# One maximum for the second layer's input, a second accumulator for the last block, and row sums for the first weight matrix

## The chip, the core and the metric

The kernel runs on one core of one Trainium2 chip. The metric is the device time of one execution in microseconds (us). A core has five engines that run on their own and meet through semaphores: TensorE (PE, with its weight loads PEld), VectorE (DVE), ScalarE (ACT), GpSimd (POOL) and SyncE (SP, which only issues transfers here).

## The reference

The input x has 2 sequences of 4096 tokens with 192 features. A causal convolution over 7 tokens, whose taps are a softmax over one row of weights per head, is followed by two feed-forward layers of width 2048: the first with a sigmoid-approximated GELU, the second with a rational function P/Q.

```python
w = exp(weight - max(weight)); w = w / (sum(w) + 1e-9)      # 8 heads, 7 taps
x = einsum('hk,bskhg->bshg', w, x_unf)                      # 8192 x 192
h = x @ w_in1;  g = h / (1 + exp(-1.702 * h));  x2 = g @ w_out1
h = x2 @ w_in2
P = a0 + a1*h + a2*h**2 + a3*h**3
Q = 1 + abs(b0)*abs(h) + abs(b1)*h**2
out = (P / (Q + 1e-6)) @ w_out2
```

All weights of the two layers, the taps' softmax and both layers belong to the program. The weight matrices come as 64-bit floats and are turned into 32-bit ones on DVE.

## The kernel before, in words

The 8192 tokens are worked on in 16 blocks of 512. A block's 512 x 192 input is held transposed as one tile of 128 x 768: 512 columns with features 0 to 127 (bank 0 where it is in PSUM, the accumulators) and 256 columns in which features 128 to 191 of the two halves of the block stand above each other (bank 1). Precision comes from splitting: a 32-bit operand is scaled by a power of two and kept as a high and a low 16-bit part, and a product is three 16-bit products (`TERMS`). So before a layer's input can be split, the largest magnitude in it has to be known: DVE makes a maximum per partition, PE spreads it over all partitions with a small matmul (`all_max`, L85), DVE takes the maximum of that (L89) and makes the power of two (`scales`, L78 to L348), ACT writes the high part (`high`, L333), DVE the low part (`low`, L336). For x2, the second layer's input, four more small DVE operations (`x2_scales`, L343) make the factors of the polynomial in between.

The loop is a software pipeline. Phase j (0 to 14) has a front phase and a back phase. In the front phase block j + 1 goes through the first layer's input product (`h_product(0, ...)`: 12 matmuls of `h_main`, L400, and 12 of `h_side`, L413) and its GELU (ACT, L491; POOL and DVE split the result, L501 and L507), while block j goes through the second layer's input product (`h_product(1, ...)`) and the parts of the rational function (`unit`, L544 to L547; `denominator`, L552). In the back phase PE makes block j + 1's first-layer output, x2: all `o1_main` matmuls (L463, into bank 0), then all `o1_side` matmuls (L473, into bank 1 of the same tile). Meanwhile ACT takes logarithms (L558) and then inverses (L562) of block j's denominators, DVE multiplies them in (`quotient`, L566), and POOL makes the convolution of a block further ahead (`x_conv_pool`: per tap a pair of multiplications, L326, and an addition, L330) in phases 0 to 12. The second layer's output, `o2_chunk` (L452), takes one quotient's half at a time; three chunks of a block stand in the back phase, the other 13 are spread over the next front phase (`late_pe`).

The order on each engine is the order in which this code issues the instructions; no scheduler changes it. PSUM has two pools: `ps_h`, three tiles that all input products and small matmuls share in turn, and `ps_o`, one tile. x2 of a block and the output of a block take turns in that one tile: the output may start when x2 has been split, and the next x2 when the output has been copied out by `store`.

In the back phase before (L684 to L721), `x2_red(n1, 0)` takes the maximum of bank 0 after the main matmuls, and `x2_red(n1, 1)` that of bank 1 after the side matmuls; `x2_red_end` (L517) joins them. The tracker of waits goes by tiles. `all_max` stands between the two halves of the next block's `h_main` (L425 to L428). The four first quotients follow the low part.

`last_phase` (L607) works on block 15 alone: `units` makes products and polynomial, with the leftover chunks of block 14 in between, `store(j - 1)` copies block 14's output out, and only then may `own(i)`, block 15's chunks, go into the same `ps_o` tile. Five units come ahead of the first logarithms.

`prologue` (L723) loads and converts the weights. For the first matrix (three pieces) DVE makes `w_max` per piece (L195); for the others ACT makes row sums of magnitudes (`w_sum`, L203), which bound the maximum from above. `softmax_taps` (L111) stands between two steps of the first piece.

## Time and profile before

| what | us |
|---|---|
| median of three runs | 1273.59 |
| the runs | 1272.25, 1273.59, 2085.2 |
| profiled execution | 1266.0 |
| its span, first to last instruction | 1264.0 |
| mean granted TensorE clock in it | 0.993 |

The profile is of one execution. Times in it count from the span's start. A matmul in 32 bits shows as two records and its end is modelled, so starts are the better measure of PE's steps. In brackets behind a row stands how long the engine was idle before it and what ended that.

### The profile page before, as it was taken

How to read it: one execution, taken by the hardware profiler on the slowest of the kernel's cores; microseconds unless marked ns; L12 is line 12 of the kernel's file. 1: busy time of each engine (PE TensorE's matmuls, PEld its weight loads, DVE VectorE, ACT ScalarE, POOL GpSimd, SP SyncE). 2: the span in 40 equal slices, each digit the busy share in tenths (PEclk: the TensorE clock that was granted, in tenths of full speed). 3: DMA queues.
4: the chain of work that ended last, by engine and by line, in shares of the span. 5: the costliest groups of instructions: out<-in, count | busy, mean ns of one | idle time of the engine just before them, and what ended most of it. 6: DMA issues, size and time to landing. Idle time of an engine off the chain costs nothing.

```text
span 1264.0 us, 24525 instructions
## 1 busy us (share of the span) xinstructions
PE 1204.1 (95%) x10762; PEld 959.3 (76%) x10762; DVE 1049.3 (83%) x1095; ACT 828.0 (66%) x825; POOL 495.7 (39%) x400
## 2 busy tenths in 40 slices
PE   5999999999999999999999999999999999999897
PEld 3547686887868688786878868687886868788686
DVE  7888898797979879797987979799797979879485
ACT  3625857668585765858576585867658576775774
POOL 2023725427272454727345272734527263112000
PEclk9999999999999999999999999999999999999898
DMA  8710001000010001000010000100000000000000
GB/s 236 236 25 2 1 1 26 1 27 1 1 27 1 26 1 27 2 1 26 1 26 2 26 1 2 26 1 26 2 19 8 1 14 1 13 1 14 1 14 13
DMA packets 32947, 27.88 MB, mean 22 GB/s; under 512 B 10485, under 2 KB 32073, under 8 KB 32073
## 3 DMA queue, kind: packets, MB, share of 16 engines
q1 hardware_dynamic: 32248, 26.31, 7.3%
q8 instruction: 84, 1.38, 0.5%
q14 instruction: 22, 0.18, 0.0%
q10 hardware_dynamic: 593, 0.01, 0.0%
HBM read 18.97 MB, written 6.29 MB: 20 GB/s over the span
## 4 chain that ended last, share of the span: by engine, by line
PE 84%; DVE 12%; ACT 2%; issue 2%; DMA 1%; ACTq 0%; DVEq 0%
PE po L452 25%; PE ph L400 23%; PE po L463 13%; PE ph L413 12%; PE po L473 7%; DVE pp L566 3%; DVE sc L343 1%; PE pc L316 1%; DVE xs L336 1%; PE pm L85 1%; DVE v L167 1%; DVE red L512 1%; PE pt L270 1%; DVE v L176 1%; DVE top L89 1%
## 5 line engine op out<-in xcount | busy, mean ns | idle before, releaser
L501 POOL TENSOR_SCALAR hl<-g,sc 128x1024 f16<-128x1024 f32 x120 | 210.8, 1756 | 540.1 <-ACT g L491 540.1
L400 PE MATMUL ph<-xs,wm 128*128 128x256 f16 x3072 | 382.2, 274 | 3.5 <-ACT xs L333 2.2
L400 PEld LDWEIGHTS <-wm 128*128 128x128 f16 x3072 | 287.3, 98 | 75.2 <-issue 38.4
L452 PE MATMUL po<-wo,pp 128*128 128x192 f32 x1920 | 331.9, 328 | 9.5 <-DVE pp L566 9.5
L452 PEld LDWEIGHTS po<-wo,pp 128*128 128x128 f32 x1920 | 311.5, 191 | 13.7 <-PE ph L400 8.3
L491 ACT ACTIVATE g<-ph,sc 128x1024 f32<-128x1024 f32 x120 | 133.7, 1114 | 176.3 <-PE ph L413 176.1
L544 ACT ACTIVATE qq<-ph,sc 128x1024 f32<-128x1024 f32 x128 | 142.5, 1113 | 158.2 <-PE ph L400 85.6
L552 DVE SCALAR_TENSOR_TENSOR qq<-qq,ab 128x1024 f32<-128x1024 f32 x128 | 209.5, 1637 | 0.0
L413 PE MATMUL ph<-xs,wr 64*128 64x256 f16 x3072 | 194.6, 271 | 0.8 <-DVE xs L336 0.8
L507 DVE SCALAR_TENSOR_TENSOR hl<-g,sc,hl 128x1024 f16<-128x1024 f32 x120 | 180.4, 1503 | 0.0
L566 DVE SCALAR_TENSOR_TENSOR pp<-pp,ab,qq 128x1024 f32<-128x1024 f32 x120 | 179.5, 1525 | 0.0
L546 DVE TENSOR_TENSOR pp<-pp,ph 128x1024 f32<-128x1024 f32 x120 | 145.5, 1212 | 39.4 <-ACT pp L545 39.4
L413 PEld LDWEIGHTS <-wr 64*128 64x128 f16 x3072 | 138.1, 94 | 47.4 <-issue 33.0
L463 PE MATMUL po<-hl,wo 128*128 128x512 f16 x720 | 157.8, 379 | 0.0
L547 DVE SCALAR_TENSOR_TENSOR pp<-pp,sc,ph 128x1024 f32<-128x1024 f32 x120 | 153.7, 1281 | 4.3
L330 POOL TENSOR_TENSOR xc<-xc,tap 128x768 f32<-128x768 f32 x78 | 152.6, 1956 | 6.5
L558 ACT ACTIVATE qq<-qq,eps,ab 128x1024 f32<-128x1024 f32 x128 | 146.9, 1228 | 3.4 <-DVE qq L552 3.2
L545 ACT ACTIVATE pp<-ph,sc 128x1024 f32<-128x1024 f32 x120 | 143.8, 1198 | 0.2 <-PE po L452 0.2
L463 PEld LDWEIGHTS <-wo 128*128 128x128 f16 x720 | 70.3, 98 | 81.7
L562 ACT ACTIVATE qq<-qq 128x1024 f32<-128x1024 f32 x128 | 124.5, 1046 | 0.2
L326 POOL TENSOR_SCALAR tap<-xt,wt 128x512 f32<-128x512 f32 (+1 forms) x156 | 101.4, 662 | 6.4
L473 PE MATMUL po<-hl,wo 128*64 128x256 f16 x1440 | 81.5, 273 | 21.6 <-DVE red L512 21.6
(96 smaller groups left out, 700.1 us busy)
## 6 DMA issues: line engine op xcount, KB each, us to landing
raw<-in_moe_w_out_dram SPq DMA_DIRECT2D x8, 768.0 KB
out_dram<-on SPq DMA_DIRECT2D x15, 384.0 KB
xn<-in_x_dram SPq DMA_DIRECT2D x16, 256.0 KB
raw<-in_moe_w_in_dram SPq DMA_DIRECT2D x4, 1024.0 KB
xn<-in_x_dram SPq DMA_DIRECT2D x32, 64.0 KB
raw<-in_moe_w_in_dram SPq DMA_DIRECT2D x4, 512.0 KB
wr<-wr SPq DMA_DIRECT2D x8, 128.0 KB
out_dram<-on SPq DMA_DIRECT2D x2, 192.0 KB
```

Source lines behind the costliest of these rows:

```text
L330: nc.gpsimd.tensor_tensor(out=flat_of(c), in0=flat_of(c), in1=flat_of(d), op=ALU.add)
L400: nc.tensor.matmul(out=ph[:, h, k * TH:(k + 1) * TH], lhsT=wm[m][:, a_, f], rhs=xs[:, b_, h * TH:(h + 1) * TH], start=(start and k == 0 an ...
L413: nc.tensor.matmul(out=ph[:, h, k * TH:(k + 1) * TH], lhsT=wr[m][rows, a_, other, f], rhs=xs[rows, b_, T:W], start=(start and other == 0 a ...
L452: nc.tensor.matmul(out=dst, lhsT=tokens(t, k, g // 2)[:, g % 2 * P:(g % 2 + 1) * P], rhs=rhs, start=(done == 0 and g % 2 == 0 and q == 0), ...
L463: nc.tensor.matmul(out=po_t[0, n][:, 0].rearrange("p (h t) -> p h t", h=2), lhsT=w[:, 0:P], rhs=all_tokens(t, k), start=(at == 1 and q == ...
L473: nc.tensor.matmul(out=po_t[0, n][h * D2:(h + 1) * D2, 1, 0:TH], lhsT=w[:, P:D], rhs=tokens(t, k, h), start=(at == 1 and q == 0), stop=(at ...
L501: nc.gpsimd.tensor_scalar(out=hl[:, 0], in0=g, scalar1=sc1_t[n][:, 4:5], scalar2=1.0, op0=ALU.mult, op1=ALU.mult)
L507: nc.vector.scalar_tensor_tensor(out=hl[:, 1], in0=g, scalar=sc1_t[n][:, 4:5], in1=hl[:, 0], op0=ALU.mult, op1=ALU.subtract)
L547: nc.vector.scalar_tensor_tensor(out=pp, in0=pp, scalar=sc[:, 5:6], in1=h, op0=ALU.add, op1=ALU.mult)
L552: nc.vector.scalar_tensor_tensor(out=qq, in0=qq, scalar=ab[:, 14:15], in1=qq, op0=ALU.add, op1=ALU.mult)
L558: nc.scalar.activation(out=qq, in_=qq, func=ACTF.Ln, scale=ab[:, 15:16], bias=eps)
L566: nc.vector.scalar_tensor_tensor(out=pp, in0=pp, scalar=ab[:, 0:1], in1=qq, op0=ALU.add, op1=ALU.mult)
```

## The change

Four things, in the order of the program.

1. Prologue: `softmax_taps` is issued ahead of the first weight piece, and the three maxima of the first matrix (`w_max` on DVE) become row sums (`w_sum` on ACT).
2. Back phase: the two maxima of x2 and the operation that joins them become one maximum over all 768 columns, after the side matmuls. `x_scales` and `x_scale_out` of the next x move ahead of the side matmuls. The first four inverses and the first quotient move ahead of the maximum. `all_max` moves from the middle of `h_main` to its end.
3. In the back phase of block 14 (where there is no next block) ACT copies x2 out of PSUM first; maximum, high and low part read the copy, and the first chunk of block 14's output goes ahead of `all_max`.
4. `last_phase`: block 15's output gets a tile of its own from `ps_h`. Leftover chunks are spread anew, the first logarithms are of four units instead of five, own chunks come ahead of `store(j - 1)`.

```diff
     def h_product(m, n, i, between=None):
...
-            h_main(*at, start=True, chunks=(0,))
+            h_main(*at, start=True)
             if between is not None:
                 between()
-            h_main(*at, chunks=(1,))
             h_side(*at, stop=True)
...
-        if done == 0:
+        if (m, n) not in po_t:
             po_t[m, n] = ps_o.tile([P, 2, 512], F32, tag="o", name="po")
...
+    def x2_red(src):
+        red = tiny.tile([P, 1], F32, tag="red2", name="red2")
+        nc.vector.tensor_reduce(out=red, in_=flat_of(src), axis=AX.X, op=ALU.max, apply_absolute_value=True)
+        return red
...
         def units(i, late=0):
             pp = hl_tile().rearrange("p two t -> p (two t)").bitcast(F32)
             unit(j, h_product(1, j, i), pp)
-            if i < first:
-                late_step(j - 1, i)
+            late_step(j - 1, i)
...
-        first = NS // 2 + 1
-        for i, late in enumerate((0, 0, 2, 5)):
+        first = NS // 2
+        for i, late in enumerate((0, 0, 2, 1, 2, 2)):
             units(i, late)
-        units(first - 1, len(late_pe))
         each(log, j, range(first))
+        units(first + 2, 1)
+        each(inverse, j, range(first))
+        each(quotient, j, range(first - 1))
+        units(first + 3, len(late_pe))
+        quotient(j, first - 1)
+        po_t[1, j] = ps_tile("po")
+        for i in range(first):
+            own(i)
         store(j - 1)
-        for i in range(first):
+        each(log, j, range(first, NS))
+        for i in range(first, NS):
             inverse(j, i)
             quotient(j, i)
-        units(first), units(first + 1)
-        own(0)
-        units(first + 2)
-        for i in range(1, first):
-            own(i)
-        quotients(range(first, NS))
         for i in range(first, NS - 1):
             own(i)
...
     def back_phase(j, n1, n2, conv, splits):
...
-        for i in range(NS):
-            o1_product(o1_main, n1, i, splits[i])
-            log(j, i)
-        if conv is not None:
-            x_max(conv)
-        x2_red(n1, 0, red)
-        for i in range(NS):
-            o1_product(o1_side, n1, i, splits[i])
-        if conv is not None:
-            x_scales(conv)
-            x_scale_out(conv)
-        x2_red(n1, 1, red)
-        x2_red_end(red)
+        for part in (o1_main, o1_side):
+            for i in range(NS):
+                o1_product(part, n1, i, splits[i])
+                if part is o1_main:
+                    log(j, i)
+            if part is o1_main and conv is not None:
+                x_max(conv)
+                x_scales(conv)
+                x_scale_out(conv)
+        chunks = [lambda i=i, k=k: o2_chunk(j, i, k) for i in range(NS) for k in range(2)]
+        each(inverse, j, (0, 1, 2, 3))
+        quotient(j, 0)
+        src = po_t.pop((0, n1))
...
+        if n2 is None:
+            copy = p1.tile([P, 2, T], F32, tag="xc", name="copy")
+            nc.scalar.activation(out=flat_of(copy), in_=flat_of(src), func=ACTF.Copy)
+            src = copy
+        red = x2_red(src)
+        if n2 is None:
+            chunks.pop(0)()
+            all_max(red, pm)
+        else:
+            early[n2, 0] = h_product(0, n2, 0, lambda: all_max(red, pm))
             early[n2, 1] = h_product(0, n2, 1)
...
-        x2_split(n1, sc, sc1_t.pop(n1)[:, 6:7])
-        each(quotient, j, (0, 1, 2, 3))
+        x2_split(n1, src, sc, sc1_t.pop(n1)[:, 6:7])
+        each(quotient, j, (1, 2, 3))
...
+        softmax_taps()
         w_high(("in", 0, 0))
-        softmax_taps()
...
-        w_max(("in", 0, 0), red[:, 0:1])
+        w_sum(("in", 0, 0), red[:, 0:1])
```

On PE, in a steady back phase, after the last main matmul, where `pm` is the tile of the next x's maximum. Before:

```order
L463 MATMUL po<-hl_2092,wo_82 128x512
L85 MATMUL pm<-ident,red 128x128 [waits Activation_49]
L473 LDWEIGHTS wo_82
L473 MATMUL po<-hl_1617,wo_82 64x256 [waits DVE_49]
L473 LDWEIGHTS wo_82
```

Now:

```order
L457 MATMUL po<-hl_2091,wo_82 128x512
L85 MATMUL pm<-ident,red 128x128 [waits Activation_49]
L467 LDWEIGHTS wo_82
L467 MATMUL po<-hl_1616,wo_82 64x256
L467 LDWEIGHTS wo_82
```

The order is the same (L473 is now L467); the first side matmul's wait for DVE is gone.

On DVE, in the same back phase, from the next x's scale (`sc_2201`, then `sc_2199`) to the quotients; `sc_2311` belongs to x2. Before:

```order
L348 TENSOR_SCALAR sc_2201<-sc_2201 128x1 [waits DVE_49]
L512 TENSOR_REDUCE red_2141<-po 128x1
L343 TENSOR_SCALAR sc_2201<-sc_2201,cst 128x1
...
L343 TENSOR_SCALAR sc_2201<-sc_2201,cst 128x1 [waits DVE_49]
L512 TENSOR_REDUCE red_2141<-po 128x1 [waits PE_49]
L517 TENSOR_SCALAR red_2141<-red_2141 128x1 [waits DVE_49]
L89 TENSOR_REDUCE top<-pm_2310 128x1 [waits PE_49]
...
L343 TENSOR_SCALAR sc_2311<-ab,sc_2311 128x3 [waits DVE_49]
...
L336 SCALAR_TENSOR_TENSOR xs_2372<-po,sc_2311,xs_2372 128x768 [waits Activation_49]
L566 SCALAR_TENSOR_TENSOR pp<-pp,ab,qq 128x1024 x4
```

Now:

```order
L338 TENSOR_SCALAR sc_2199<-sc_2199,cst 128x1 [waits DVE_49]
L557 SCALAR_TENSOR_TENSOR pp<-pp,ab,qq 128x1024 [waits Activation_49]
L507 TENSOR_REDUCE red_2312<-po 128x1 [waits PE_49]
L89 TENSOR_REDUCE top<-pm_2310 128x1 [waits PE_49]
...
L338 TENSOR_SCALAR sc_2311<-ab,sc_2311 128x3 [waits DVE_49]
...
L331 SCALAR_TENSOR_TENSOR xs_2370<-po,sc_2311,xs_2370 128x768 [waits Activation_49]
L557 SCALAR_TENSOR_TENSOR pp<-pp,ab,qq 128x1024 x3
```

One quotient (L566, now L557) has moved ahead of the maximum (L512, now L507), which is one row where there were three.

On ACT, at the turn from block 14 to block 15, from the first inverses of block 14 to the first pass over block 15. Before:

```order
L562 ACTIVATE qq<-qq 128x1024 [waits Activation_49] x4
L333 ACTIVATE xs_12806<-po,sc_12795 128x768 [waits DVE_49,PE_49]
L562 ACTIVATE qq<-qq 128x1024 [waits Activation_49] x4
L544 ACTIVATE qq<-ph,sc_12795 128x1024 [waits DVE_49,PE_49,Activation_49]
L545 ACTIVATE hl_12834<-ph,sc_12795 128x1024
```

Now:

```order
L553 ACTIVATE qq<-qq 128x1024 [waits Activation_49] x4
L691 ACTIVATE copy<-po 128x768 [waits PE_49]
L328 ACTIVATE xs_12785<-copy,sc_12769 128x768 [waits DVE_49,Activation_49]
L553 ACTIVATE qq<-qq 128x1024 x4
L535 ACTIVATE qq<-ph,sc_12769 128x1024 [waits DVE_49,PE_49]
```

The copy stands behind the four inverses, and the high part (L333, now L328) reads it.

## Rows read from the trace of the kernel before

**Rows 1.** The page, busy times: share of the span and instructions of each engine.
```profile
PE 1204.1 (95%) x10762; PEld 959.3 (76%) x10762; DVE 1049.3 (83%) x1095; ACT 828.0 (66%) x825; POOL 495.7 (39%) x400
```
**Rows 2.** Waits of PE: who was waited for, us in total, times, longest.
```profile
PE po L473 <- DVE red L512: 21.6, 15, 1.5
```
**Rows 3.** Timeline of PE, one back phase: start, length, line, tile, count, idle before.
```profile
442.11 5.43 PE L473 MATMUL po<-hl,wo 128*64 128x256 f16 x96 [1.55 <-DVE red L512]
447.47 0.83 PE L400 MATMUL ph<-xs,wm 128*128 128x256 f16 x6
448.31 0.49 PE L85 MATMUL pm<-ident,red 128*128 128x128 f32 x2
...
450.14 1.49 PE L400 MATMUL ph<-xs,wm 128*128 128x256 f16 x12
451.56 1.49 PE L413 MATMUL ph<-xs,wr 64*128 64x256 f16 x24
...
454.90 3.33 PE L452 MATMUL po<-wo,pp 128*128 128x192 f32 x19 [0.44 <-DVE pp L566]
```
**Rows 4.** Timeline of PE, the turn to the last block and the end.
```profile
1188.93 6.09 PE L452 MATMUL po<-wo,pp 128*128 128x192 f32 x24 [4.28 <-DVE pp L566]
...
1228.96 2.84 PE L452 MATMUL po<-wo,hl 128*128 128x192 f32 x16 [1.80 <-DVE hl L566]
...
1249.55 10.40 PE L452 MATMUL po<-wo,hl 128*128 128x192 f32 x48 [5.16 <-DVE hl L566]
```
**Rows 5.** Timeline of ACT, inverses in that phase and in phase 14.
```profile
443.74 3.90 ACT L562 ACTIVATE qq<-qq 128x1024 f32<-128x1024 f32 x4
...
1181.83 2.93 ACT L562 ACTIVATE qq<-qq 128x1024 f32<-128x1024 f32 x3
```
**Rows 6.** Timeline of POOL, the phase of rows 3.
```profile
444.35 1.14 POOL L326 TENSOR_SCALAR tap<-xt,wt 128x512 f32<-128x512 f32 x2
445.58 1.82 POOL L330 TENSOR_TENSOR xc<-xc,tap 128x768 f32<-128x768 f32 x1
```
**Rows 7.** Timeline of DVE, the same phase and the x maximum after it.
```profile
447.58 0.42 DVE L512 TENSOR_REDUCE red<-po 128x1 f32<-128x256 f32 x1 [4.91 <-PE po L473]
...
449.84 0.71 DVE L343 TENSOR_SCALAR sc<-ab,sc 128x3 f32<-128x3 f32 x1
...
450.99 1.01 DVE L336 SCALAR_TENSOR_TENSOR xs<-po,sc,xs 128x768 f16<-128x768 f32 x1
451.92 2.84 DVE L566 SCALAR_TENSOR_TENSOR pp<-pp,ab,qq 128x1024 f32<-128x1024 f32 x1
...
479.79 0.94 DVE L358 TENSOR_REDUCE red<-xn 128x1 f32<-128x768 f32 x1
```
**Rows 8.** Timeline of DVE, phase 14, where POOL rests.
```profile
1185.96 0.47 DVE L343 TENSOR_SCALAR sc<-sc 128x2 f32<-128x2 f32 x2
...
1187.50 4.86 DVE L566 SCALAR_TENSOR_TENSOR pp<-pp,ab,qq 128x1024 f32<-128x1024 f32 x4
```
**Rows 9.** Timeline of DVE, first back phase, two operations that met POOL.
```profile
142.26 1.71 DVE L552 SCALAR_TENSOR_TENSOR qq<-qq,ab 128x1024 f32<-128x1024 f32 x1
...
153.79 2.11 DVE L343 TENSOR_SCALAR sc<-sc 128x2 f32<-128x2 f32 x2
```
**Rows 10.** Timeline of POOL, first back phase.
```profile
141.36 2.96 POOL L326 TENSOR_SCALAR tap<-xt,wt 128x512 f32<-128x512 f32 x2
...
153.82 1.81 POOL L330 TENSOR_TENSOR xc<-xc,tap 128x768 f32<-128x768 f32 x1
```
**Rows 11.** One stretch: us, busy PE, PEld, DVE, ACT, POOL, granted clock, DMA, GB/s.
```profile
1189.00:1195.00 6.00, 6.00 (x26) 5.77 (x28) 3.37 (x3) 1.32 (x2) 0.00 (x0) 0.68 0.00 0
```
**Rows 12.** The beginning: the taps' transfer in the chain, and DVE's timeline.
```profile
4.39 5.58 DMA wt<-in_weight_dram
...
9.01 0.69 DVE L164 TENSOR_SCALAR u<-raw 128x1024 uint32<-128x1024 uint32 x1 [0.44 <-DMA raw<-in_moe_w_in_dram]
...
13.48 1.22 DVE L195 TENSOR_REDUCE wred<-v 128x1 f32<-128x1024 f32 x1
```

More of the change, by code (lines that the diff above doesn't have):

```diff
@@ L616, in units, with own @@
             denominator(j, i)
-        def quotients(steps):
-            each(log, j, steps)
-            for i in steps:
-                inverse(j, i)
-                quotient(j, i)
-        def own(i):
+        def own(i, groups=range(NG)):
             for k in range(2):
-                o2_chunk(j, i, k)
-        first = NS // 2 + 1
-        for i, late in enumerate((0, 0, 2, 5)):
+                o2_chunk(j, i, k, groups)
+        first = NS // 2
+        for i, late in enumerate((0, 0, 2, 1, 2, 2)):
             units(i, late)
-        units(first - 1, len(late_pe))
         each(log, j, range(first))
+        units(first + 2, 1)
[6 more added lines that the diff above has]
+            own(i)
         store(j - 1)
-        for i in range(first):
+        each(log, j, range(first, NS))
+        for i in range(first, NS):
             inverse(j, i)
             quotient(j, i)
-        units(first), units(first + 1)
-        own(0)
-        units(first + 2)
-        for i in range(1, first):
-            own(i)
-        quotients(range(first, NS))
         for i in range(first, NS - 1):
@@ L645, in last_phase @@
         for groups in (range(0, 2), range(2, 4)):
-            for k in range(2):
-                o2_chunk(j, NS - 1, k, groups)
+            own(NS - 1, groups)
         store_half(j, 0)
@@ L675, in front_phase, with x2_split @@
         return splits
-    def x2_split(n, sc, unit):
+    def x2_split(n, src, sc, unit):
         xs = xs_t[1, n] = p2.tile([P, 2, W], F16, tag="xs2", name="xs2")
-        po = po_t.pop((0, n))
-        high(po, sc[:, 1:2], xs)
+        high(src, sc[:, 1:2], xs)
         x2_scales(sc, unit)
-        low(po, sc[:, 1:2], xs)
+        low(src, sc[:, 1:2], xs)
     def back_phase(j, n1, n2, conv, splits):
@@ L689, in back_phase @@
                 x_conv_pool(conv, k)
-        red = tiny.tile([P, 3], F32, tag="red2", name="red2")
-        for i in range(NS):
-            o1_product(o1_main, n1, i, splits[i])
-            log(j, i)
-        if conv is not None:
-            x_max(conv)
-        x2_red(n1, 0, red)
-        for i in range(NS):
-            o1_product(o1_side, n1, i, splits[i])
-        if conv is not None:
-            x_scales(conv)
-            x_scale_out(conv)
-        x2_red(n1, 1, red)
-        x2_red_end(red)
+        for part in (o1_main, o1_side):
[11 more added lines that the diff above has]
+        src = po_t.pop((0, n1))
         pm = ps_tile("pm2")
         sc = sc2_t[n1] = tiny.tile([P, 24], F32, tag="sc2", name="sc2")
-        if n2 is not None:
-            early[n2, 0] = h_product(0, n2, 0, lambda: all_max(red[:, 2:3], pm))
+        if n2 is None:
[8 more added lines that the diff above has]
+            early[n2, 0] = h_product(0, n2, 0, lambda: all_max(red, pm))
             early[n2, 1] = h_product(0, n2, 1)
-        else:
-            all_max(red[:, 2:3], pm)
-        each(inverse, j, (0, 1, 2, 3))
         scales(pm, sc)
-        x2_split(n1, sc, sc1_t.pop(n1)[:, 6:7])
-        each(quotient, j, (0, 1, 2, 3))
+        x2_split(n1, src, sc, sc1_t.pop(n1)[:, 6:7])
+        each(quotient, j, (1, 2, 3))
         each(inverse, j, (4, 5, 6, 7))
-        chunks = [lambda i=i, k=k: o2_chunk(j, i, k) for i in range(NS) for k in range(2)]
         if n2 is not None:
@@ L756, in prologue @@
             more()
-            w_max(("in", 0, c), red[:, c:c + 1])
+            w_sum(("in", 0, c), red[:, c:c + 1])
         w_scale(red, 3, 0)
@@ L838, in prologue @@
         x_conv_matmul(1, 1)
-        red = tiny.tile([P, 3], F32, tag="red2", name="red2")
-        x2_red(0, 0, red)
-        x2_red(0, 1, red)
-        x2_red_end(red)
+        x2 = po_t.pop((0, 0))
+        red = x2_red(x2)
         sc = sc2_t[0] = tiny.tile([P, 24], F32, tag="sc2", name="sc2")
-        all_max(red[:, 2:3], pm)
+        all_max(red, pm)
         scales(pm, sc)
-        x2_split(0, sc, cst[:, 3:4])
+        x2_split(0, x2, sc, cst[:, 3:4])
         for m in range(2, 2 * K):
```

10 lines of the change are left out of this document (removed).

## The prediction, made before the changed kernel was run

> **What bounds the kernel now.** I read the page's busy times first: PE is busy for 95% of the span [rows 1]. So time is won where PE stands still, or where it runs at the lower clock. The list of PE's waits comes next: the longest entry is the wait of the second half of a first-layer output product (L473) for DVE's first maximum (L512), 15 times, 21.6 us in all [rows 2]. Then the timelines of one steady back phase (phase 4, 440 to 455 us), engine by engine, to see which end comes last. On PE the reader sees two holes: 1.55 us ahead of L473 and 0.44 us ahead of the first L452, which waits for the first quotient (L566) [rows 3]. The first hole is not work: the maximum reads one bank of the accumulator and L473 writes the other, but both carry one tile name, so PE waits for a DVE operation that itself stands behind the scale of the next x. Last I read the end of the program, where PE stands for 4.28, 1.80 and 5.16 us [rows 4].
>
> **The steady phase, step by step.** Before, PE goes from the start of its hole, 442.11 − 1.55 = 440.56, to its first output chunk at 454.90: 14.34 us [rows 3]. After the change the same work, in the new order, is: 5.36 for the 96 side matmuls (442.11 to 447.47), 1.42 for the next product's main part, 0.33 for the maximum's matmul (0.49 with its tail), 0.71 + 1.42 + 0.71 for the rest of this product and the next, 0.71 + 1.42 for the second-layer product (main 450.14 to 451.56; the 24 side rows at 451.56 are two sides). That is 12.08, with some 0.1 for changes of data type 12.2. What is open is how long PE then waits for DVE, at two places.
>
> First place, the maximum's matmul. Sides end at 440.56 + 5.36 = 445.9, PE can issue this matmul 1.42 later, at 447.3. Its operand: the first of four inverses, issued at 443.74, ends about 444.8 (four take 3.90) [rows 5]. The first quotient, now ahead of the maximum, starts then. It meets POOL, which is in a pair of tap multiplications, 444.35 to 445.49, and then in an addition of 1.82 [rows 6]. These two kinds of work exclude each other: the same quotient took 2.84 us at 451.92, until the addition beside it was over [rows 7], against steps of 1.2 us where POOL rests [rows 8]. But a waiting DVE operation gets in between the two halves of a pair: L552, issued at 142.26, needed 1.71, and the pair beside it was stretched from 1.14 to 2.96 [rows 9, 10]. So I take it that the quotient gets in at about 445.04 and ends at 446.1. The maximum over 768 elements did not stand in the trace in this form. The nearest rows are 0.94 for 768 elements out of SBUF and 0.42 for 256 out of PSUM [rows 7]; I take 0.94. It runs from 446.03 to 446.97, so PE does not wait. Bounds: 0 if so; 0.2 if the quotient has to let the whole pair pass; 2.1 if it also has to let the addition pass (ends at 447.40, quotient 448.5, maximum 449.4).
>
> Second place, the low part of the scaled x2. From the maximum's matmul to the three-element scale operation it is 1.53 (448.31 to 449.84), then two more small ones and the low part, 1.01 long, which started 2.68 after that matmul [rows 3, 7]. The matmul now stands at 447.3, so the three-element operation asks at 448.8. The quotient has pushed POOL's addition back to about 446.55 to 448.35; a pair follows from 448.45. I expect the small operations to get through between and behind its halves, the low part from 449.85 to 450.85. PE needs it 0.33 + 2.84 after the matmul and two thirds of a first half side later: 450.7. Wait: 0.2. Bounds: 0.05 if POOL does not touch them, 1.8 if one of them is caught behind an addition.
>
> The price of being caught stands in the trace: in the first back phase two small scale operations took 2.11 us, at 153.79, until the addition issued at 153.82 was over [rows 9, 10]; where POOL rested the same two took 0.47 [rows 8]. So 1.64 per capture. The Trainium skill, SBUF — State Buffer, section Terms, goes further: the port pair that DVE and GpSimd share is held for a full instruction and the loser blocks fully. By that rule any of the three locked operations behind the maximum can be caught, which would be the first rival below; the trace agrees with full blocking (2.84 and 2.11), and shows the hand-over between two instructions.
>
> The first chunk finds its quotient done since 446.1, so the 0.44 us are gone. What is queued behind the first quotient on DVE is the maximum and everything after it, and PE waits for that; this is the risk of the move. The second to fourth quotients follow the low part as before, the second done by about 452.6, and PE wants it at 452.8 + 2.6.
>
> So a phase costs 12.2 + 0.2 = 12.4 instead of 14.34: 1.95 to 2.0 less; I take 2.0, with ends 0.3 (one capture) and 2.15. Thirteen phases have the POOL convolution: 26.0. PE reaches the front phase some 1.0 us earlier against ACT and DVE; the list of PE's waits has no entry from there, so the cover is the distance by which accumulators come free ahead of PE, and I cost the shift at nothing; without that cover it is up to 1.0 a phase. Phase 13 has no convolution: its wait was half as long ((21.6 − 13 × 1.55)/2 = 0.73), and the quotient ends 0.6 after the sides, so about 0.15 comes back: 0.6.
>
> **The end.** In phase 14 the hole of 4.28 us, the maximum's matmul and its wait (some 0.5 and 0.8) lie between the sides and 1188.93, so the sides ended near 1183.4; now 0.75 earlier. ACT's four inverses end near 1184.8 (three of them from 1181.83) [rows 5]. Then come a copy (768 elements, about 0.94 as a maximum of that size), the maximum, and one chunk, which wants only the copy; the maximum's matmul stands at about 1186.9. The low part, 3.5 behind it, ends at 1190.4; before, the first quotient followed it at 1187.50 [rows 8]. The second quotient is then done at 1191.6, so PE, which has two chunks behind it, does two more until 1194.2 = U. Before, products started at 1195.0 with three chunks done [rows 4]. From U on DVE is the bound: the first result of a unit after 4.6 (estimate: a product of 2.13 and two ACT passes of 1.2, as long as a quotient's step [rows 8]), then four steps of 1.2 for four units and three for three, 30.3, then the first quotient: U + 36.2. PE has 8 products (17.1) and 12 chunks (15.6) for this time and idles some 2.3 and, for an accumulator, 1.1. Then 16 own chunks at 1.3 (two took 2.84 with their gap [rows 4]), with about 1.0 of waiting for the fifth quotient: U + 58.0 = 1252.2 for PE's end instead of 1249.55 + 10.40 = 1259.95. So 7.75 less. In this lie most of the 5.16 us stall and the half-speed that followed it: six chunks took 10.40 instead of 7.8 [rows 4]. The separate accumulator is what lets own chunks start ahead of the store.
>
> Against this: PE stands twice for 3.1 us before U, and after the stall of 4.28 us the mean granted clock from 1189 to 1195 was 0.68, part of that stretch at 1.2 instead of 2.4 GHz, three chunks in 6.09 [rows 4, 11]. I charge 1.5 (ends 0 and 4). Term: 6.2, ends 3.5 and 7.75.
>
> **The beginning.** Three maxima of 1.22 leave DVE's chain to the weights' scale, 3.66. Given back: DVE began on the weights at 9.01, now it begins with the softmax, whose taps land at 4.39 + 5.58 = 9.97, so 1.0 [rows 12]; the last of three sums stands alone on ACT, 1.2 (the nearest row is the maximum of the same size), and its way to DVE and POOL's diagonals beside DVE take some 0.3. So 1.1 earlier; ends 0 (the third weight piece lands late) and 2.8 (an early stretch at half speed falls away as well). The first and second sum lie beside DVE's next piece. The one maximum of the prologue gains nothing, since the matmul behind it stands behind convolution matmuls. The sums change scales, not instruction counts.
>
> **Sum.** 26.0 + 0.6 + 6.2 + 1.1 = 33.9. The profiled execution took 1266.0 (span 1264.0 and 2.0 around it): 1232.1. The median of the runs shown, 1273.59, stands 7.6 over it; I carry that offset: 1240. A measurement of this kernel can tell about 2% from no change, here 1248.1.
>
> **Rivals.**
> A. POOL catches the scales: in each convolution phase one small operation stands behind an addition. For it: it happened in phase 0, and the distance to the next addition is only some 0.3 us. Against it: by the sum above the request falls into a pair. Saving 2.0 − 1.7 per phase: 1273.6 − (3.9 + 7.9) = 1262. This is also the result of the port rule above taken strictly. Chance 0.17.
> B. Slower. The first quotient has lost its place to the addition and the scales too: 2.1 + 1.64 more waiting per phase against 2.0 won, 22 us over 13 phases, less 7.9: 1288. It decides from 2.6 us of waiting per phase. For it: nothing was queued ahead of the maximum before. Against it: the hand-over at 142.26. Chance 0.03.
> C. The end gives nothing, because copy, late maximum and half-speed eat it: 1246. For it: three idle stretches instead of one before U. Chance 0.06.
> D. The change doesn't do what it says, and L473 goes on waiting for DVE: 20 us of the sum gone, 1260. Against it: in the order its first row waits for nothing of DVE any more. Chance 0.02.
>
> **How the numbers follow.** Forecast 0.72, 1240, its own range 1231 to 1247. The range reaches to A: 1231 to 1262. Faster by over 2%: the forecast nearly whole and half of C, 0.72; within 2%: A, B, D, half of C and a little of the forecast, 0.26; slower 0.02.
>
> **What would show it.** Right: no wait of L473's successor for a maximum; idle on PE under 0.5 us per phase between the sides and the first chunk; the first quotient about 1.3 long; the maximum near 0.94; PE's end of the program without a stall over 3 us after the first unit. Wrong: a first quotient of over 2 us, a small scale operation of over 1 us in the steady phases, PE waiting over 1 us for the low part (then A), a maximum's matmul over 1 us behind the main part (then B), or the granted clock under 0.9 over the last 60 us (then C).

## The result, and the profile after

The changed kernel takes 1241.7 us in the median (1240.16 to 1241.92, 4 runs) against 1273.6 beside it: 0.975 of the time before, 95% interval 0.973 to 0.977. (Of four executions of the kernel before, 1272.25, 1273.59 and 1275.46 are counted, and one of 2085.2 is not.) The forecast was 1240. The profiled execution of the changed kernel took 1241.92, with a span of 1239.7.

The page, busy times, answers to [rows 1]; the list of PE's waits, after, to [rows 2]:

```profile
PE 1200.2 (97%) x10762; PEld 957.8 (77%) x10762; DVE 1024.6 (83%) x1060; ACT 832.7 (67%) x832; POOL 545.4 (44%) x400
```
```profile
PE ph L408 <- DVE xs L331: 2.0, 12, 0.2
```

The entry of 21.6 us is gone. What is late next in a steady phase is the low part of x2 (now L331), by at most 0.2. POOL is busy 49.7 us longer with the same 400 instructions. The pairs below show what this is: the pair that VectorE's quotient falls into shows 2.12 and the next one 1.15. So waiting for VectorE is counted as part of POOL's instruction.

PE in phase 4, which answers to [rows 3]:

```profile
439.93 5.43 PE L467 MATMUL po<-hl,wo 128*64 128x256 f16 x96
445.29 1.48 PE L395 MATMUL ph<-xs,wm 128*128 128x256 f16 x12
446.61 0.39 PE L85 MATMUL pm<-ident,red 128*128 128x128 f32 x2
...
450.31 0.61 PE L408 MATMUL ph<-xs,wr 64*128 64x256 f16 x8 [0.16 <-DVE xs L331]
...
452.18 3.09 PE L446 MATMUL po<-wo,pp 128*128 128x192 f32 x18
```

DVE and POOL in the same stretch, which answer to [rows 6, 7]:

```profile
444.28 1.29 DVE L557 SCALAR_TENSOR_TENSOR pp<-pp,ab,qq 128x1024 f32<-128x1024 f32 x1 [2.77 <-ACT qq L553]
445.49 0.94 DVE L507 TENSOR_REDUCE red<-po 128x1 f32<-128x768 f32 x1
...
448.05 0.59 DVE L338 TENSOR_SCALAR sc<-ab,sc 128x3 f32<-128x3 f32 x1
448.67 0.67 DVE L338 TENSOR_SCALAR sc<-sc 128x2 f32<-128x2 f32 x2
449.26 1.01 DVE L331 SCALAR_TENSOR_TENSOR xs<-po,sc,xs 128x768 f16<-128x768 f32 x1
```
```profile
443.81 2.12 POOL L321 TENSOR_SCALAR tap<-xt,wt 128x512 f32<-128x512 f32 x2
446.00 1.81 POOL L325 TENSOR_TENSOR xc<-xc,tap 128x768 f32<-128x768 f32 x1
447.91 1.15 POOL L321 TENSOR_SCALAR tap<-xt,wt 128x512 f32<-128x512 f32 x2
449.15 1.82 POOL L325 TENSOR_TENSOR xc<-xc,tap 128x768 f32<-128x768 f32 x1
```

The quotient (L557) begins at 444.28, inside POOL's pair, and stretches that pair from 1.14 to 2.12; POOL's addition starts behind it, at 446.00. The maximum takes 0.94, and its matmul follows PE's main part without a wait. The three- and two-element scale operations fall on POOL's next pair (447.91) and are through before the addition at 449.15. (The row at 448.67 joins two operations: one on two elements, which ends at 449.09, and one on a single element, which runs beside the addition.) From PE's first free moment ahead of the sides to the first output chunk it is 452.18 − 439.93 = 12.25 us, against 14.34 before.

The beginning, DVE and PE, answers to [rows 12]; the end of PE, to [rows 4]:

```profile
17.34 0.17 DVE L114 TENSOR_REDUCE mx<-wt 128x2 f32<-128x14 f32 x1 [8.80 <-DMA wt<-in_weight_dram]
```
```profile
34.24 2.92 PE L395 MATMUL ph<-xs,wm 128*128 128x256 f16 x12 [2.18 <-ACT xs L328]
...
1165.55 1.57 PE L446 MATMUL po<-wo,pp 128*128 128x192 f32 x8 [2.97 <-ACT copy L691]
...
1171.57 5.49 PE L446 MATMUL po<-wo,pp 128*128 128x192 f32 x16 [2.92 <-DVE pp L557]
1176.99 1.09 PE L408 MATMUL ph<-xs,wr 64*128 64x256 f16 x12
...
1213.49 10.64 PE L446 MATMUL po<-wo,hl 128*128 128x192 f32 x64 [2.32 <-DVE hl L557]
1225.01 10.67 PE L446 MATMUL po<-wo,hl 128*128 128x192 f32 x64 [0.88 <-DVE hl L557]
```

The taps landed 7 us later than in the trace of before, so the first product started at 34.24, against 28.18 in that trace. At the end the single stall of 5.16 us is gone, but two chunks at 1171.57 took 5.49 us, at a granted clock of 0.50, which is 1.2 instead of 2.4 GHz:

```profile
1171.60:1176.90 5.30, 5.30 (x16) 4.95 (x16) 2.30 (x2) 1.45 (x2) 0.00 (x0) 0.50 0.00 0
```

By stage, from the two profiled spans (1264.0 and 1239.7; 24.3 less). The marks are the first main matmul of the first-layer output product in a back phase (L463, now L457), and PE's end.

| stretch | before | after | difference |
|---|---|---|---|
| start to phase 0's mark | 133.31 | 140.95 | +7.64 |
| phase 0's mark to phase 13's | 961.95 | 934.99 | −26.96 |
| phase 13's mark to phase 14's | 71.40 | 70.76 | −0.64 |
| phase 14's mark to PE's end | 93.29 | 88.98 | −4.31 |

A steady phase takes 71.8 to 72.1 instead of 74.05.

### The profile page after: what moved, and what is told of

Same layout as the page of the kernel before. It is cut to its first block, busy times and chain, and to the rows that moved or that the text cites. A ratio compares the mean times of both kernels' runs of the same rounds, so it can differ in the third digit from the quotient of the medians.

```text
span 1239.7 us, 24487 instructions
## 1 busy us (share of the span) xinstructions
PE 1200.2 (97%) x10762; PEld 957.8 (77%) x10762; DVE 1024.6 (83%) x1060; ACT 832.7 (67%) x832; POOL 545.4 (44%) x400
## 4 chain that ended last, share of the span: by engine, by line
PE 84%; DVE 7%; ACT 6%; DMA 1%; issue 1%; ACTq 0%; DVEq 0%
PE ph L395 26%; PE po L446 25%; PE ph L408 13%; PE po L457 11%; PE po L467 6%; ACT qq L549 3%; PE pc L311 1%; DVE sc L338 1%; DMA wt<-in_weight_dram 1%; DVE xs L331 1%; DVE v L167 1%; PE pm L85 1%; ACT qq L553 1%; PE pt L265 1%; DVE v L176 1%
## 5 line engine op out<-in xcount | busy, mean ns | idle before, releaser
L557 DVE SCALAR_TENSOR_TENSOR pp<-pp,ab,qq 128x1024 f32<-128x1024 f32 x120 | 179.7, 1516 | 51.4 <-ACT qq L553 51.4
L543 DVE SCALAR_TENSOR_TENSOR qq<-qq,ab 128x1024 f32<-128x1024 f32 x128 | 197.3, 1541 | 0.0
L501 DVE SCALAR_TENSOR_TENSOR hl<-g,sc,hl 128x1024 f16<-128x1024 f32 x120 | 176.9, 1474 | 0.0
L325 POOL TENSOR_TENSOR xc<-xc,tap 128x768 f32<-128x768 f32 x78 | 162.8, 2087 | 6.5
L457 PE MATMUL po<-hl,wo 128*128 128x512 f16 x720 | 157.8, 379 | 0.0
L321 POOL TENSOR_SCALAR tap<-xt,wt 128x512 f32<-128x512 f32 (+1 forms) x156 | 139.5, 906 | 6.4
L457 PEld LDWEIGHTS <-wo 128*128 128x128 f16 x720 | 70.4, 98 | 81.6
L467 PE MATMUL po<-hl,wo 128*64 128x256 f16 x1440 | 81.5, 273 | 0.0
```

What stands on the lines that cost most here:

```text
L325: nc.gpsimd.tensor_tensor(out=flat_of(c), in0=flat_of(c), in1=flat_of(d), op=ALU.add)
L457: nc.tensor.matmul(out=po_t[0, n][:, 0].rearrange("p (h t) -> p h t", h=2), lhsT=w[:, 0:P], rhs=all_tokens(t, k), start=(at == 1 and q == ...
L467: nc.tensor.matmul(out=po_t[0, n][h * D2:(h + 1) * D2, 1, 0:TH], lhsT=w[:, P:D], rhs=tokens(t, k, h), start=(at == 1 and q == 0), stop=(at ...
L501: nc.vector.scalar_tensor_tensor(out=hl[:, 1], in0=g, scalar=sc1_t[n][:, 4:5], in1=hl[:, 0], op0=ALU.mult, op1=ALU.subtract)
L543: nc.vector.scalar_tensor_tensor(out=qq, in0=qq, scalar=ab[:, 14:15], in1=qq, op0=ALU.add, op1=ALU.mult)
L557: nc.vector.scalar_tensor_tensor(out=pp, in0=pp, scalar=ab[:, 0:1], in1=qq, op0=ALU.add, op1=ALU.mult)
```

## The experiments

Beside these runs, before took 1273.25 to 1273.9 in the median. Periods are those of the steady phases, from mark to mark.

**1. The kernel before, once more.** No edit. The profiled span of before was 24.3 over that of after, but the medians differ by 31.9.

> The kernel before, unchanged. Theory: in most of its executions the taps' transfers land near 17 us, as they did in the profiled execution of the changed kernel, and the execution profiled first (landing at 9.97) was a lucky one; that is the offset of 7.6 us between it and the median. Then VectorE's first operation on the taps starts near 17.3, the first product of the first layer near 34, and the whole takes 1272 to 1276. Rival: the late landing comes from the changed kernel, and the offset from something else: then the first operation on the taps starts near 10.9 again, the first product near 28.2, also where the time is over 1272.

Measured: 1273.84 (one run), DVE and PE:

```profile
9.77 1.23 DVE L167 SCALAR_TENSOR_TENSOR v<-raw,u 128x1024 uint32<-128x1024 uint32 x1
17.55 0.17 DVE L114 TENSOR_REDUCE mx<-wt 128x2 f32<-128x14 f32 x1 [6.55 <-DMA wt<-in_weight_dram]
```
```profile
34.86 0.60 PE L400 MATMUL ph<-xs,wm 128*128 128x256 f16 x4 [2.18 <-ACT xs L333]
```

The theory holds in the main: in an execution of the usual length the taps are late in the kernel before as well. The profiled execution of [rows 12], where they landed at 9.97, was the exception. Its span was 7.9 shorter than this one (1264.0 and 1271.9). Of that, 6.7 stand already at the first product (28.18 and 34.86), so they are the landing; another 0.95 comes from phase 14's mark to PE's end (93.29 and 94.24), and why is not shown. Compared with this span (1271.9), the changed kernel's is 32.2 shorter: 27.8 less in the phases, 5.3 less in the end (94.24 to 88.98), and 0.9 more up to phase 0's mark (140.0 to 140.95).

**2. The first quotient behind the low part again** (phases 0 to 13), the one maximum kept:

```diff
-        quotient(j, 0)
+        if n2 is None:
+            quotient(j, 0)
...
-        each(quotient, j, (1, 2, 3))
+        each(quotient, j, (1, 2, 3) if n2 is None else (0, 1, 2, 3))
```

> The changed kernel with its first quotient put back behind the low part in phases 0 to 13; the one maximum stays. Theory: the quotient's lead is worth more than the 0.44 us that the first chunk waited, because by holding up half of POOL's pair it also shifts POOL's next addition away from the small scale operations. Without it, POOL's pair ends near 445.0 in phase 4 and the following addition starts near 448.2, ahead of the two-element scale operation, which stands behind it until about 450.0; the low part comes about 1.2 late, PE waits 1.3 to 1.4 for it instead of 0.17, and a phase takes 73.1 to 73.4 instead of 71.9 to 72.1: some 16 us more in all, 1256 to 1260. Rival: the parts of the sum simply add; PE gets 0 to 0.45 us of waiting for the first chunk back, a phase takes 72.0 to 72.5, the whole 1243 to 1248.

Measured: 1249.8 (ratio 0.982, 0.980 to 0.984), 72.74 a phase. DVE, POOL and PE in phase 4:

```profile
449.24 1.92 DVE L338 TENSOR_SCALAR sc<-sc 128x2 f32<-128x2 f32 x2
```
```profile
449.07 1.81 POOL L325 TENSOR_TENSOR xc<-xc,tap 128x768 f32<-128x768 f32 x1
```
```profile
452.13 0.61 PE L408 MATMUL ph<-xs,wr 64*128 64x256 f16 x8 [1.06 <-DVE xs L331]
454.00 1.30 PE L446 MATMUL po<-wo,pp 128*128 128x192 f32 x7
```

Between both ranges. The mechanism is the theory's: the two small operations take 1.92 instead of 0.67, because POOL's addition began 0.17 ahead of them (449.07), and PE waits 1.06 for the low part. No first chunk waits. The theory put the price too high: it is 0.7 to 0.9 a phase, not 1.2.

**3. The maximum's matmul back in the middle of the main part:**

```diff
-            h_main(*at, start=True)
+            h_main(*at, start=True, chunks=(0,))
             if between is not None:
                 between()
+            h_main(*at, chunks=(1,))
```

> The changed kernel with the maximum's matmul back between the two halves of the main part, 0.71 us earlier. Theory: the maximum ends as before near 1.15 after the sides, so the matmul waits 0.5 to 0.7 there in each steady phase, and the wait of 0.17 for the low part goes, since this chain starts no earlier while PE comes later: a phase takes 72.3 to 72.6, the whole 1246 to 1250. Rival: the place makes no difference, because the low part's end sets the phase in either order: 71.9 to 72.1 a phase, 1240 to 1243.

Measured: 1243.6 (0.977, 0.975 to 0.980; the profiled run 1243.47), 72.11 a phase. PE in phase 4:

```profile
448.46 0.49 PE L85 MATMUL pm<-ident,red 128*128 128x128 f32 x2 [0.35 <-DVE red L508]
```

Nearer to the rival. The matmul waits 0.35, but the wait for the low part is gone, and the phase is 0.0 to 0.3 longer, 2.3 from phase 0's mark to phase 13's (937.29 against 934.99). So in phases with POOL's work the new place is worth little, at most 0.3 of the 2.0. In phase 13, which has none, it is worth all that was won there: from its mark to the next this run takes 71.41, as before (71.40), against 70.76. The same matmul in phase 13, in the changed kernel and here:

```profile
1093.53 0.46 PE L85 MATMUL pm<-ident,red 128*128 128x128 f32 x2 [0.29 <-DVE red L507]
```
```profile
1096.82 0.46 PE L85 MATMUL pm<-ident,red 128*128 128x128 f32 x2 [0.95 <-DVE red L508]
```

This run is also a control for the end, where the program is the changed kernel's. The two stalls are the same, and the two chunks behind them run at full speed:

```profile
1169.48 1.57 PE L447 MATMUL po<-wo,pp 128*128 128x192 f32 x8 [2.96 <-ACT copy L692]
...
1175.49 2.87 PE L447 MATMUL po<-wo,pp 128*128 128x192 f32 x16 [2.92 <-DVE pp L558]
```

2.87 against 5.49, and from phase 14's mark to PE's end 86.61 against 88.98. So the half-speed stretch cost 2.6 at these chunks. At PE's end 2.4 of it show, where this run has a shorter stretch of its own among its last chunks (granted clock 0.50 from 1215.4 to 1218.8).

**4. The two maxima again, the quotient still ahead** (phases 0 to 13): the maximum over each bank, the first between main and side matmuls, and their combination, as before the change.

```diff
+            if part is o1_main and n2 is not None:
+                x2_red_part(n1, 0, red)
...
         quotient(j, 0)
+        if n2 is not None:
+            x2_red_part(n1, 1, red)
+            x2_red_end(red)
```

> The changed kernel with the two maxima over half the accumulator each, as before, in phases 0 to 13: the first between the main and the side matmuls, so the sides wait for it again; the first quotient stays ahead of the second maximum. Theory: what small DVE operations cost behind the maximum is set by where POOL's addition then stands. The sides' wait of 1.55 comes back and moves the scales later by as much, the three-element operation then asks about 450.3 (by the clock of before's phase 4), while POOL, pushed back by the quotient as in the changed kernel, adds from 449.7 to 451.5: caught, 0.5 to 0.9 more of waiting for the low part. A phase takes 73.9 to 74.4, no less than before's 74.05, the whole 1267 to 1274. Rival: the parts add, only the wait of 1.55 returns: a phase takes 73.4 to 73.6, the whole 1260 to 1264.

Measured: 1267.1 (0.994, 0.993 to 0.996), 74.00 a phase. DVE, POOL and PE:

```profile
455.57 0.20 DVE L338 TENSOR_SCALAR sc<-sc,sc 128x1 f32<-128x1 f32 x1
455.81 1.32 DVE L338 TENSOR_SCALAR sc<-ab,sc 128x3 f32<-128x3 f32 x1
```
```profile
455.29 1.81 POOL L325 TENSOR_TENSOR xc<-xc,tap 128x768 f32<-128x768 f32 x1
```
```profile
447.68 5.43 PE L467 MATMUL po<-hl,wo 128*64 128x256 f16 x96 [1.54 <-DVE red L506]
...
458.62 0.61 PE L408 MATMUL ph<-xs,wr 64*128 64x256 f16 x8 [0.71 <-DVE xs L331]
```

As the theory had it: the sides wait 1.54 again, the three-element operation stands behind POOL's addition (1.32), and PE waits 0.71 for the low part. With experiment 2 the square is full. Its first corner is the kernel before, which also has the maximum's matmul in the middle of the main part; experiment 3 puts that place at 0.0 to 0.3.

| us a phase | two maxima | one maximum |
|---|---|---|
| quotient behind the low part | 74.05 | 72.74 |
| quotient ahead | 74.00 | 71.8 to 72.1 |

The one maximum is worth 1.3 by itself, the quotient's lead 0.05 by itself, both together 2.0 to 2.2.

**5. The taps first:** the four early loads of weights on ScalarE's queue behind the taps, the second block of x later.

```diff
-        more(), more(), more(), more()
-        x_load(1)
+        for _ in range(4):
+            more(nc.scalar)
```

> The changed kernel with the four early loads of weight pieces issued behind the taps on ScalarE's queue, instead of on SyncE's beside them, and the second block of x loaded after the first piece is used. Theory: the taps (hundreds of packets of 28 bytes or less) land late only because they share the DMA engines with packets of the weights; alone they land by 8 to 10 us, and the main part of phase 0, which started at 140.95 in the changed kernel, starts at 131 to 135; the whole takes 1231 to 1236. Rival: the small packets take that long by themselves; the taps land at 15 to 18 as before and the weights later still: the main part of phase 0 starts at 141 to 146, the whole takes 1241 to 1247.

Measured: 1234.1 (0.969, 0.968 to 0.971). DVE and PE:

```profile
8.56 0.17 DVE L114 TENSOR_REDUCE mx<-wt 128x2 f32<-128x14 f32 x1
...
11.27 0.17 DVE L119 TENSOR_REDUCE sm<-wt 128x2 f32<-128x14 f32 x1 [2.33 <-ACT wt L118]
```
```profile
28.65 0.60 PE L396 MATMUL ph<-xs,wm 128*128 128x256 f16 x4 [2.18 <-ACT xs L329]
```

The taps are there by 8.56 without a wait, the first product starts 5.6 earlier, phase 0's mark stands at 133.77 instead of 140.95, and the whole is 7.6 shorter. (The other 1.6 up to the mark are a stretch at half speed that this execution does not have; the last part comes back to it.) So the taps were late because the weights, and behind them the second block of x, were on the DMA engines beside them; which of the two counts was not tried apart. The Trainium skill, DMA: Bandwidth & Descriptors, section Queues, rings and completion order, says that each DMA engine takes turns between the queues that it has work for, a packet at a time. By that rule small packets on one queue would each stand behind a packet of the other. The runs agree as far as they show it: the taps' 256 packets of 28 bytes lie between 2.9 and 16.6 us in the changed kernel and between 2.9 and 6.1 us here.

**6. The kernel before with the taps first.** The same edit in before: what is the new beginning worth when the taps are early?

> The kernel before with the taps first on ScalarE's queue and the four early weight loads behind them, as in e4_taps_first. It tells what the beginning of the change (sums instead of maxima, taps ahead of the first piece) is worth when the taps are not late: e4_taps_first started its first product at 28.65 and needed VectorE until 24.04 for the three pieces. Theory: nothing there, since VectorE then waits for the landing of the third piece (until 19.5) in either order, and what the maxima cost lies in that wait: first product at 28.4 to 29.2, the whole 1264 to 1268 . Rival, the prediction's sum: the three maxima of 1.22 stand in the chain, less what the order gives back: first product at 29.6 to 31.5, the whole 1266 to 1270.

Measured: 1270.0 (0.997, 0.996 to 0.998). DVE and PE:

```profile
11.89 0.69 DVE L165 TENSOR_SCALAR u<-raw 128x1024 uint32<-128x1024 uint32 x1 [3.20 <-DMA raw<-in_moe_w_in_dram]
```
```profile
31.06 0.71 PE L401 MATMUL ph<-xs,wm 128*128 128x256 f16 x4 [2.18 <-ACT xs L334]
```

The rival, so the prediction's way of reckoning, with more than its 1.1: 31.06 − 28.65 = 2.4 us earlier with sums and taps ahead. The theory, that the landing of the third piece hides the maxima, falls. With late taps it is only 34.86 − 34.24 = 0.6, of which 0.2 is the landing itself (17.55 and 17.34), since the first piece's high part, which before was done while DVE waited for the taps (9.77 in experiment 1), now stands behind them.

**7. The end as before:** before's order of the last block and of its output chunks, no copy, no quotient ahead in phase 14; the late maximum kept.

```diff
-            copy = p1.tile([P, 2, T], F32, tag="xc", name="copy")
-            nc.scalar.activation(out=flat_of(copy), in_=flat_of(src), func=ACTF.Copy)
-            src = copy
...
-        for i, late in enumerate((0, 0, 2, 1, 2, 2)):
+        first = NS // 2 + 1
+        for i, late in enumerate((0, 0, 2, 5)):
```

> The changed kernel with the end of the program as before: no copy and no first quotient ahead in phase 14 (its one maximum reads the accumulator), and the last block in before's order (five units, all quotients before the own chunks, its chunks in the accumulator that the store frees). Theory, the prediction's own working: the new end is worth 6.2 without the charge of 1.5 for the clock being borne out exactly; from the start of phase 14's main part to TensorE's end it took 88.98 in the changed kernel and 93.29 to 94.24 before, of which 0.8 is the late maximum, kept here: 92.5 to 93.5 from there to TensorE's end, the whole 1245 to 1247. Rival: the new order is worth nothing and the 4.3 us come from the one maximum and from where the half-speed stretches fall: 89 to 91, the whole 1241 to 1243.

Measured: 1244.1 (0.975, 0.973 to 0.977; single runs 1239.5 to 1245.7). In its profiled execution (1245.68) phase 14's mark to PE's end takes 94.16, and the old stalls are back:

```profile
1162.10 0.49 PE L85 MATMUL pm<-ident,red 128*128 128x128 f32 x2 [1.05 <-DVE red L507]
1166.87 7.04 PE L446 MATMUL po<-wo,pp 128*128 128x192 f32 x24 [4.28 <-DVE pp L557]
```

By the trace the new end is worth 94.16 − 88.98 = 5.2 us, more in the theory's direction than expected. The time shows less of it, 3.8 between the profiled executions and 2.4 between the medians, in part because this execution's phases 1 to 12 were 2.1 us shorter than those of the changed kernel's: all of them were of the shorter kind that the last section describes (71.80). Time alone would not have separated theory and rival. The run takes the new end away as a whole; what the copy, the second accumulator and the new order are worth each by itself is not shown.

**8. The copy ahead of three inverses**, on top of experiment 5:

```diff
-        each(inverse, j, (0, 1, 2, 3))
+        each(inverse, j, (0, 1, 2, 3) if n2 is not None else (0,))
...
             src = copy
+            each(inverse, j, (1, 2, 3))
```

> e4_taps_first with ScalarE's copy of the last accumulator issued behind the first of the four inverses of phase 14, instead of behind all four. Theory: the copy, the first chunk and the maximum come 2.2 us earlier, and the second to fourth inverse end 0.8 later, still ahead of the second quotient; PE's wait for the copy goes from 2.97 to under 0.9, the end of the program comes 2 to 3 us earlier, and up to 2.4 more where the shorter standstill leaves the clock whole: 1228 to 1232. Rival: nothing of it reaches the end, since the later inverses hold up the second quotient and with it VectorE's chain that sets the end: 1233.5 to 1235.

Measured: 1231.3 (0.966, 0.965 to 0.968). PE:

```profile
1156.17 1.57 PE L447 MATMUL po<-wo,pp 128*128 128x192 f32 x8 [0.90 <-ACT copy L692]
1157.58 0.38 PE L85 MATMUL pm<-ident,red 128*128 128x128 f32 x2
```

The theory holds. The wait for the copy goes from 2.96 in experiment 5 to 0.90, and from phase 14's mark to PE's end it is 86.15 instead of 89.49, 3.3 less. Part of that is the clock's: the chunk behind this wait takes 1.57 here and took 2.58 there.

**9. The taps' loads split over both queues**, on top of 8: two on ScalarE's, four on SyncE's ahead of the weights, the loads of a and b later.

> e7t_copy_taps with the taps' loads split over both queues (two on ScalarE's, four on SyncE's ahead of the weights), the weights back on SyncE's queue, and the loads of a and b behind the second block of x. Theory: VectorE no longer waits 2.1 us for ScalarE, whose table load stood behind the weights' issue, and the third weight piece is issued 1.4 us earlier: the first product starts at 26.5 to 28 instead of 28.65, the whole is 0.7 to 2 us under e7t_copy_taps. Rival: the taps' small packets meet the weights again and land late, 10 to 17: first product from 29 on, the whole 1 to 7 us over e7t_copy_taps.

Measured: 1229.2 (0.965, 0.963 to 0.966), 2.2 under experiment 8, a little more than the theory's 0.7 to 2; the first product starts at 27.18, as the theory said:

```profile
27.18 0.60 PE L398 MATMUL ph<-xs,wm 128*128 128x256 f16 x4 [2.18 <-ACT xs L331]
...
1159.15 5.49 PE L449 MATMUL po<-wo,pp 128*128 128x192 f32 x16 [2.92 <-DVE pp L560]
1164.58 1.16 PE L411 MATMUL ph<-xs,wr 64*128 64x256 f16 x12
```

The last two lines show what was left at the end: PE waits for the second quotient, does its two chunks, and only then begins the products of the last block, on whose first result DVE's whole remaining chain stands.

**10. The first two products of the last block ahead of these chunks**, on top of 9:

```diff
-        for f in chunks[:3]:
+        now = 3 if n2 is not None else 1
+        for f in chunks[:now]:
...
-        for i, late in enumerate((0, 0, 2, 1, 2, 2)):
+        for i, late in enumerate((0, 2, 2, 1, 2, 2)):
```

> e8_taps_split with the first two products of the last block ahead of the two chunks of phase 14's second quotient (those chunks then follow the second product). Theory: VectorE sets the end from the first unit of the last block on, and its start is only held up by TensorE, which stands 2.9 us for the second quotient and then does two chunks at half speed with the scaled x2 long ready; the first product starts at the low part, 6 to 7.5 us earlier, the first VectorE operation of a unit as well, the end 5 to 7.5 us earlier: 1221.5 to 1225. Rival: what is won ahead of the first unit is given back, because TensorE then lacks accumulators or the late chunks and has to catch up before its own chunks: under 2 us, 1227.5 to 1229.5.

Measured: 1226.2 (0.963, 0.961 to 0.964), the fastest version of the study, 15.5 us under the changed kernel. PE:

```profile
1158.70 0.39 PE L411 MATMUL ph<-xs,wr 64*128 64x256 f16 x4 [0.67 <-ACT xs L331]
1159.75 0.61 PE L411 MATMUL ph<-xs,wr 64*128 64x256 f16 x8 [0.66 <-DVE xs L334]
```

Between theory and rival. From phase 14's mark DVE's first operation of a unit comes 6.7 us earlier, PE's end 4.6 (86.97 to 82.40). Of the 2.1 between, 1.0 was lost before the last block's own chunks began, and 1.1 behind that, where some of these chunks ran at half speed. The profiled spans differ by only 2.8 (1227.4 and 1224.6), since this execution reached phase 0's mark 2.2 later (134.52 against 132.31); the medians differ by 2.95.

## Why the prediction was right, point by point

**The steady phase: right, term by term.** Predicted 26.0 for the thirteen phases with POOL's work; measured 26.96. The steps held too: the quotient in POOL's pair (444.28 to 445.57; phase 4 began 0.57 earlier than before, so that is 444.85 to 446.14 on before's clock, where about 445.04 to 446.1 was expected), 0.94 for the maximum, no wait for its matmul, 0.16 for the low part (expected 0.2), and 12.25 us from hole to chunk (12.4). The hand-over of [rows 9, 10], a waiting DVE operation getting in between two POOL instructions, happens in all twelve phases behind phase 0. In phase 0 the quotient meets an addition and takes 2.14, the maximum's matmul waits 0.56 for it, and the phase is still 2.0 shorter. Experiments 2 and 4 show what the prediction only half saw: it counted the quotient's lead as 0.44 won and a risk, and the push on POOL's addition only as a step of the timing, while this push is what the lead is worth. The gains don't add: 1.3 and 0.05 make 2.0 or more.

Phase 13: the number right by luck. Predicted 0.6, measured 0.64, but not by the hole of 0.73 less 0.15. The maximum comes no earlier than before, since the quotient stands ahead of it: its matmul starts 17.59 behind the mark in both kernels and waits 0.29 for it. What is won is the half of the main part that PE now does ahead of this matmul; with the matmul in the middle nothing is left (71.41 in experiment 3). Without the quotient's lead the phase takes 70.23 (experiment 2), so here the lead costs 0.5.

Rival A needed a capture in each phase. The price it named was near (1.64 there; 1.92 − 0.47 = 1.45 in experiment 2, with the 0.47 of [rows 8], and 1.32 − 0.23 = 1.1 in experiment 4, with 0.23 for the three-element operation alone, as in phase 13), the place was not. Of the three operations that the prediction calls locked, the last, on one element, was not held: 0.21 beside an addition. Within a capture the two runs agree with full blocking, the rule of the Trainium skill, SBUF — State Buffer, section Terms: the caught operations end within 0.03 of POOL's additions (450.91 and 450.88; 457.12 and 457.10).

**The beginning: the step that failed.** The prediction took "taps land at 9.97" from one execution, and that one was an exception; in the other runs with this order of the loads VectorE had them at 17.3 to 19.9. The new beginning was to be worth 1.1. It gave 0.6 at the first product with late taps and 2.4 with early ones, and in the profiled execution another 1.6 were lost on the way to phase 0, where a stretch ran at half speed (clock 0.98 from 60 to 140 us, 1.00 in experiments 1 and 2; experiment 2, with the same beginning and its taps at 17.36, reached phase 0's mark at 139.38 instead of 140.95):

```profile
60.00:140.00 80.00, 78.26 (x544) 46.55 (x544) 63.90 (x90) 35.99 (x39) 19.76 (x12) 0.98 0.11 31
```

**The offset: right, without a cause.** The 7.6 us between the profiled execution and the median were carried over as they were. Had they been left out, the forecast would have been 1232, some 10 too low. Experiment 1 puts 6.7 of it down to the taps' landing, and experiment 5 shows what makes them late. Why they were early once is open.

**The end: mechanism right, the clock's charge too low.** By the prediction the products start U = 11.5 after the sides and PE ends U + 58.0. Measured: 1176.99 = U, own chunks from U + 36.5 (36.2 predicted), PE's end at 1235.68 = U + 58.7. U itself came 14.4 behind the sides' end; the low part and the second quotient were where they were expected (7.7 and 8.9 behind the sides), the two chunks took 5.4 instead of the 2.6 counted. So the charge of 1.5 for the clock should have been 2.4 to 2.6 (experiment 3). The term, 6.2, came out at 4.3 between the two profiled executions and 5.3 against experiment 1.

**Together:** 33.9 predicted, 32.2 between executions with the same landing of the taps, 31.9 between the medians. Against experiment 1 the phases gave 27.8 (26.6 predicted), the end 5.3 (6.2) and the beginning −0.9 (1.1). So the forecast is this near in part by luck, since the misses of +1.2, −0.9 and −2.0 partly cancel; the large term is near because the place where each operation meets POOL came out as worked out. Two figures of the working are off without consequence: the maximum is started at 446.03, 0.07 ahead of the quotient's end, and 25 steps of 1.2 make 30.0 and not 30.3.

## What to carry to other kernels

Where two engines exclude each other, an edit moves the meetings too: work out for every small operation behind the moved one what the other engine is doing at that moment, and test parts of a change together as well as alone. A transfer's landing in one profile is one draw; profile the kernel twice before a step rests on it. Where an engine's chain sets the end, look what its first input waits for: in experiment 10 a change of order alone brought that input 6.7 us nearer and the end 4.6.

## What the runs showed that was not expected

- A few small packets can hold up the start: the taps were there by 8.56 alone and at 17.3 to 19.9 beside the weights, with 9.97 once.
- The same two stalls (2.97 and 2.92; 2.96 and 2.92) were followed by half speed in the changed kernel and by full speed in experiment 3. What decides it was not tried.
- Operations on one element pass beside POOL's addition (0.20 at 455.57), on two or three elements they wait for its end (1.32 for the one on three; 1.92 for the one on two, with a one-element operation of 0.21 behind it).
- The steady phases of the changed kernel come in two lengths, 71.83 and 72.08. In the longer ones the quotient takes 1.55 instead of 1.29 and everything behind it is later by that, because it asks earlier in the first half of POOL's pair and waits for that half's end; in experiments 5, 7 and 10 it takes 1.28 or 1.29 in every one, and the phases 71.80. Why POOL is later in some phases was not followed. DVE in a longer phase:

```profile
875.78 1.55 DVE L557 SCALAR_TENSOR_TENSOR pp<-pp,ab,qq 128x1024 f32<-128x1024 f32 x1 [2.76 <-ACT qq L553]
```
